# A ReLU² feed-forward behind an attention on one Trainium2 core: batch 0's first z tiles moved from SBUF to SBUF, and a new order of work

## The chip, the cores and the metric

The kernel runs on one core of one Trainium2 chip. The metric is the time of one execution on the device in microseconds (us). A profile of one execution stands beside the times; in it PE is the matrix engine (TensorE), PEld its weight loads, DVE is VectorE, ACT is ScalarE, POOL is GpSimd and SP is SyncE, which here only issues DMAs.

## The reference

There are 8 batches (b) with 8 heads each, a sequence of 512 tokens and 32 state rows per head, head size 64. Each head's x attends to the state, and the state attends to x; both results go through one feed-forward of width 512 → 2048 → 512 with a squared ReLU.

```python
scores = scale * x @ state.T;   a  = softmax(scores);   xread = a @ state      # 512 rows a head
scores2 = scale * state @ x.T;  a2 = softmax(scores2);  sread = a2 @ x         # 32 rows a head
x = concat([xread, sread])          # per batch 544 rows of 8*64 = 512
out = (maximum(x @ w_in, 0) ** 2) @ w_out
```

The weights come as 64-bit floats: the kernel reads them as pairs of 32-bit words and makes 32-bit floats of them on the chip.

## The kernel before

Everything that PE multiplies in quantity is split into a high and a low part (`_hi`, `_lo`), and a product is three matmuls: high by high, high by low, low by high. One matmul with 512 columns is the unit of the long run.

For the 512 token rows of a batch, `xread @ w_in` is not formed from xread. The state rows are multiplied into w_in first: `z = state @ w_in`, and then `h = a @ z`. So there are these pieces of work:

- **Weights.** `w_tile(fc)` loads one of 16 tiles of w_in (512 KB, `w_raw`) and `singles` makes `wi` of it; `wo_tile(fc)` does the same for w_out (`wo_raw`, `wof`) and splits the result into `wo_hi`, `wo_lo`. All raw tiles share four buffers (tag `raw`). `singles` takes one ACT instruction (L355) and three DVE instructions (L359, L364, L370) for a tile of 128x512.
- **Scores.** `scores(b, g)` for the two groups g of a batch: batches 0 and 1 in plain 32-bit matmuls (`sq`, L569, with the padded state `sp_f` that `pad` makes), the others with split x (`xt_hl`, `pq`, L590). A softmax on DVE, ACT and POOL follows, then `a_hi` and `a_lo`. In batches 0 and 1 PE turns tiles over (`sT`, `pa`).
- **z.** `z_part(k, g)` makes z for batches 0 to 3 and 256 columns of w_in: eight matmul records (`pz`, L471), two ACT copies to `z_stage`, one DMA from ACT's queue to `zd` in DRAM. `z_fetch(b, k)` reads a batch's z back with four DMAs on SP's queue (`z_raw`) and splits it into `z_hi`, `z_lo`. Only the first 256 columns of batch 0 go another way: `z_direct` (L495, `pzd`) multiplies the padded state with w_in again, straight into the layout that is needed. Batches 4 to 7 get theirs from `z_quad` (L441) and `zq`.
- **Up and down.** For each of the 16 columns tiles fc of a batch, `up` makes `ph` (six matmuls, L779), then ACT and DVE form r, the square and `g_hi`, `g_lo`; `down` adds twelve matmuls (L815) into four PSUM tiles `po`. Batch 0 is done in two visits (`PARTS`): fc 0 to 5, then all of batch 1, then the rest of batch 0.
- **Read.** `read(b, g)` makes the state rows' results (`pt`, `pr`, `sr`), and at the end 16 more `up` and `down` steps handle them.

Nothing is issued in the order of the code. Each piece is recorded with its engine, an assumed cost, its buffers and a due time, and `Planner` lays all of them out in an assumed timeline: an engine that comes free takes, of the pieces that could begin at once, the one that is due first. The order that comes of it is the fixed order of each engine's queue on the chip. `plan` computes due times backwards from the `up` and `down` steps, with a slack (`SLACKS`) on every step; `run` tries 16 such plans (four `FIRST` by four `SLACKS`) and keeps the one that ends first in its own account. A DMA waits at the head of its queue (SP's or ACT's) until its buffers are free, and what is queued behind it waits too.

`keep_busy(k)` is filler: four small matmuls on a constant tile (`warm`, written to a PSUM tile of tag `ph`). There are 40 of them (160 matmuls, L842); the planner puts them where PE would have nothing else in its account. On the chip they run wherever they stand.

Of the kernel before, what the change touches and what calls it, by code (L numbers as in the profile page):

```python
# [44 lines left out]
class Planner:  # L45


    RATE = 330.0
    NEAR = 1.0
    SLACKS = (1.0, 1.5, 2.0, 2.5)  # L50

    def __init__(self):
        self.ops, self.last_w, self.readers, self.chains = [], {}, {}, {}
        self.whens = []

    def op(
        self, engs, run, r=(), w=(), lat=0.2, due=1e9, begin=0.0, size=0, both=False, hold=None,
        chain=None, land=2.2, slack=0.3, unit=None,
    ):
# [75 lines left out]
    def plan(self, scale):  # L135
# [26 lines left out]
        while len(log) < len(self.ops):  # L162
# [80 lines left out]
def memory_attention_then_relu2_ffn(  # L243
# [77 lines left out]
    ]  # L321
    zd = [dr.tile([P, NG, HG, FW], F32, name=f"zd_{k}") for k in range(NFCH)]
# [25 lines left out]
    def singles(out_f, words, r, w):  # L348

        bits = lambda: out_f().bitcast(I32)  # L350
        high = lambda: words()[..., 1]
        low = lambda: words()[..., 0]
        n = 512
        op(
            act(n, 0.08), lambda e: nc.scalar.activation(out_f(), high().bitcast(F32), AF.Abs, scale=GUARD),  # L355
            r=r, w=w,
        )
        op(
            dve2(n), lambda e: nc.vector.tensor_scalar(  # L359
                out=bits(), in0=bits(), scalar1=3, scalar2=None, op0=ALU.logical_shift_left),  # L360
            r=w, w=w,
        )
        op(
            dve(n), lambda e: nc.vector.scalar_tensor_tensor(  # L364
                out=bits(), in0=high(), scalar=-0x80000000, in1=bits(),
                op0=ALU.bitwise_and, op1=ALU.bitwise_or),
            r=[*r, *w], w=w, both=True,
        )
        op(
            dve(n), lambda e: nc.vector.scalar_tensor_tensor(  # L370
                out=bits(), in0=low(), scalar=29, in1=bits(),
                op0=ALU.logical_shift_right, op1=ALU.bitwise_or),
            r=[*r, *w], w=w, both=True,
        )
# [56 lines left out]
    def z_quad(kq, g, q, w_hl, begin):  # L431
# [15 lines left out]
        op(("PE", 0.75), products, r=r, w=pz, begin=begin)  # L447
# [3 lines left out]
    def z_store(pz, stage, out, keys, part, order):  # L451
        for i in range(2):
            op(
                act(512), lambda e, i=i: nc.scalar.copy(out=part(i), in_=pz[i].t),
                r=[pz[i]], w=[(stage, i)],
            )
        load(
            out, lambda: stage.t.rearrange(order), 512,
            r=[(stage, 0), (stage, 1)], w=keys, eng="ACT", issue=0.35, hold=None, land=4.5,
        )  # L460

    def z_part(k, g):
# [3 lines left out]
        def product(e):  # L466
            for q in range(NQ):
# [41 lines left out]
    def z_fetch(b, k):  # L509
# [3 lines left out]
        for j in range(HG):  # L513
            load(
                lambda j=j: raw.t[j * N:(j + 1) * N], lambda j=j: src[:, :, j, :], 64,
                r=[("zd", b // GB, k, g, q) for g in range(NG) for q in range(NQ)], w=[(raw, j)], issue=0.62, hold=30.0, chain="zf",
            )
# [9 lines left out]
    def pad(b):  # L527
        pairs[b] = [tile_([P, NG, S], F32R, n) for n in ("a_hi", "a_lo")]
        src = stP[b].rearrange("p (g q n) -> p g q n", g=NG, q=2)
        rows = [slice(i * D, (i + 1) * D) for i in range(2)]  # L530
        at = [slice(i * N, (i + 1) * N) for i in range(2)]
        raw = tile_([P, NG, 2, N], F32, "sp_raw")
        load(lambda: raw.t, lambda: src, 64, w=[raw], due=1e9 if b else -60.0)
        for i in range(2):
            if b < PLAIN_X:
                if i == 0:
                    wide[b] = tile_([P, NG, 2, P + D], F32, "sp_f1", "x_hl") if b else sp_f
                    if b:
                        op(("POOL", 0.9), lambda e: nc.gpsimd.memset(wide[b].t, 0.0), w=[(wide[b], 0), (wide[b], 1)])
                op(  # L540
                    dve2(2 * N * NG), lambda e, i=i: nc.vector.tensor_copy(
                        out=wide[b].t[rows[i], :, :, at[i]], in_=raw.t[rows[i]]),
                    r=[raw], w=[(wide[b], i)],
                )
                continue
# [7 lines left out]

    def scores(b, g):
        xt = tile_([P, NQ, S], F32, "xt_raw", "xraw")
        load(
            lambda: xt.t, lambda: xT[b, g * CG:(g + 1) * CG, :].rearrange("(q p) s -> p q s", p=P),
            512, w=[xt], chain="x", due=1e9 if b else -12.0 + 4 * g, eng="SP" if b or g else "ACT",
        )
# [4 lines left out]
        if b < PLAIN_X:  # L564
            sq = tile_([P, S], F32, "sq", "px")

            def product(e):
                for q in range(NQ):
                    nc.tensor.matmul(  # L569
                        sq.t, lhsT=wide[b].t[:, g].rearrange("p q n -> p (q n)")[:, q * P:(q + 1) * P],  # L570
                        rhs=xt.t[:, q, :], start=q == 0, stop=q == NQ - 1,
                    )

            op(("PE", 1.77), product, r=[(wide[b], i) for i in range(2)] + [xt], w=[sq])
            pst = tile_([P, S], F32, "st")
            op(act(S), lambda e: nc.scalar.copy(out=pst.t, in_=sq.t), r=[sq], w=[pst])
        else:
            pst = tile_([P, S], F32, "st")
            for q in range(NQ):
# [3 lines left out]
                    [xt], [(hl, 0)], [(hl, 1)], engs=[gps(S)],  # L583
# [27 lines left out]
        turned = b < PLAIN_X  # L611
# [143 lines left out]
    def wo_tile(fc):  # L755
# [4 lines left out]
            w=[raw],  # L760
# [76 lines left out]
    def keep_busy(k):  # L837
# [6 lines left out]
        op(("PE", 0.4), product, w=[ph], begin=1.2 + 0.4 * k)  # L844
# [47 lines left out]
    for b, lo, hi in PARTS:  # L892
        if b not in started:
            pad(b)
            for g in range(NG):
                scores(b, g)
            started.add(b)
        if lo == 0 and b >= 1:
# [120 lines left out]
```

## Time and profile before

| | |
|---|---|
| median of 3 executions | 687.50 us (687.41 to 688.02) |
| profiled execution | 687.25 us, of it 685.5 us from the first to the last instruction (the span) |
| PE | 676.1 us busy, 99% of the span, granted clock 0.999 |
| DVE, ACT, POOL | 417.7, 398.1 and 158.4 us busy |
| DMA | 79.55 MB, on average 116 GB/s |

A row of a timeline gives start, duration, engine, source line and operation, tiles out<-in, and in brackets the engine's idle time ahead of it with what ended it. Matmuls overlap: a matmul of 512 columns has a duration of about 0.39 us, but the next one starts 0.23 us later, and it is this step from start to start that the sums use.

### The profile page before, as it was taken

To read this page: it belongs to the slowest core of one execution; us is meant where nothing else is said; L and a number is where in the kernel's file an instruction comes from. 1 tells how busy PE (TensorE), PEld (TensorE's weight loads), DVE (VectorE), ACT (ScalarE), POOL (GpSimd) and SP (SyncE) were. 2 spreads that over 40 slices of the span, in tenths; PEclk is the share of its full clock that TensorE was granted. 3 is DMA by queue.
4 is the path that set the end of the run, shared out by engine and by line. 5 is a ranking of instruction groups with operands and counts; after the bars stand their busy time and mean duration, and the time that the engine had idled before them with its cause. 6 is when DMAs were issued, how large, how long until landed. Compare 5 with 4: busy or idle time off the path is not lost.

```text
span 685.5 us, 9700 instructions
## 1 busy us (share of the span) xinstructions
PE 676.1 (99%) x3288; PEld 540.5 (79%) x3288; DVE 417.7 (61%) x716; ACT 398.1 (58%) x758; POOL 158.4 (23%) x175
## 2 busy tenths in 40 slices
PE   8999999999999999999999999999999999999997
PEld 6677777788878887777777888888888888888895
DVE  6999898475486666554454675775954444333532
ACT  4897778585555667565444665675754443334452
POOL 1010022233333444111210552354413210000000
PEclk9999999999999999999999999999999999999999
DMA  9967984451132213523242223221232112100101
GB/s 312 362 221 246 328 277 146 153 181 64 62 123 67 93 31 138 203 109 143 72 174 92 85 69 105 81 89 55 92 124 63 31 32 93 31 1 0 62 1 32
DMA packets 50609, 79.55 MB, mean 116 GB/s; under 512 B 6528, under 2 KB 32896, under 8 KB 50560
## 3 DMA queue, kind: packets, MB, share of 16 engines
q1 hardware_dynamic: 45488, 61.37, 27.7%
q10 hardware_dynamic: 5072, 17.57, 6.5%
q8 instruction: 26, 0.43, 0.3%
q14 instruction: 23, 0.19, 0.1%
HBM read 52.17 MB, written 26.74 MB: 115 GB/s over the span
## 4 chain that ended last, share of the span: by engine, by line
PE 90%; DVE 6%; DMA 2%; issue 1%; ACT 0%; SPq 0%; DVEq 0%; ACTq 0%
PE po L815 53%; PE ph L779 28%; PE pr L720 2%; PE pz L441 2%; PE pq L590 2%; PE pz L471 2%; PE pt L702 1%; DVE wi L364 1%; DVE wi L370 1%; DVE wi L359 1%; DMA w_raw<-w_in 1%; DMA xt_raw<-xT 1%; DMA z_raw<-zd 1%; DVE wof L364 0%; DVE wof L370 0%
## 5 line engine op out<-in xcount | busy, mean ns | idle before, releaser
L815 PE MATMUL po<-wo_hi,g_hi 128*128 128x512 f32 x544 | 218.0, 401 | 0.0
L815 PE MATMUL po<-wo_lo,g_hi 128*128 128x512 f32 x544 | 213.9, 393 | 0.0
L793 DVE TENSOR_TENSOR ph<-ph,r 128x512 f32<-128x512 f32 (+1 forms) x111 | 76.2, 686 | 197.5 <-ACT r L785 197.1
L815 PE MATMUL po<-wo_hi,g_lo 128*128 128x512 f32 x544 | 155.8, 397 | 0.0
L785 ACT ACTIVATE r<-ph 128x512 f32<-128x512 f32 (+1 forms) x144 | 82.7, 575 | 104.1 <-PE ph L779 103.5
L339 ACT CAST g_hi<-ph 128x512 fp32r<-128x512 f32 (+1 forms) x144 | 81.2, 564 | 99.6 <-PE po L815 94.5
L815 PEld LDWEIGHTS po<-wo_hi,g_hi 128*128 128x128 f32 x544 | 102.3, 188 | 28.1 <-issue 7.3
L815 PEld LDWEIGHTS po<-wo_lo,g_hi 128*128 128x128 f32 x544 | 102.4, 188 | 20.8 <-issue 0.2
L815 PEld LDWEIGHTS po<-wo_hi,g_lo 128*128 128x128 f32 x544 | 99.6, 188 | 22.6 <-issue 2.4
L344 DVE TENSOR_TENSOR g_lo<-ph,g_hi 128x512 fp32r<-128x512 f32 (+1 forms) x144 | 94.0, 653 | 29.2 <-PE po L815 21.9
L344 POOL TENSOR_TENSOR xn_hl<-xn_raw,xn_hl 128x512 fp32r<-128x512 f32 x32 | 44.2, 1381 | 175.9 <-ACT xn_hl L339 147.4
L779 PE MATMUL ph<-a_hi,z_hi 128*128 128x512 f32 x256 | 80.5, 395 | 1.2 <-DVE g_lo L344 1.2
L779 PE MATMUL ph<-a_hi,z_lo 128*128 128x512 f32 x256 | 80.1, 394 | 0.0
L779 PE MATMUL ph<-a_lo,z_hi 128*128 128x512 f32 x256 | 79.1, 390 | 0.0
L779 PEld LDWEIGHTS ph<-a_hi,z_hi 128*128 128x128 f32 x256 | 47.8, 188 | 12.4 <-ACT wo_hi L339 1.5
L779 PEld LDWEIGHTS ph<-a_lo,z_hi 128*128 128x128 f32 x256 | 48.0, 188 | 11.4
L779 PEld LDWEIGHTS ph<-a_hi,z_lo 128*128 128x128 f32 x256 | 48.0, 188 | 11.3
L344 DVE TENSOR_TENSOR z_lo<-z_raw,z_hi 128x512 fp32r<-128x512 f32 x63 | 48.6, 772 | 2.0 <-ACT z_hi L339 1.5
L344 POOL TENSOR_TENSOR xt_hl<-xt_raw,xt_hl 128x512 fp32r<-128x512 f32 x24 | 32.9, 1370 | 62.3 <-ACT xt_hl L339 62.3
L339 ACT CAST z_hi<-z_raw 128x512 fp32r<-128x512 f32 x63 | 38.8, 616 | 1.8 <-DMA z_raw<-zd 1.6
L649 POOL TENSOR_TENSOR q<-q,s 128x512 f32<-128x512 f32 x13 | 13.7, 1051 | 66.1 <-DVE s L644 45.8
L339 ACT CAST xn_hl<-xn_raw 128x512 fp32r<-128x512 f32 x32 | 19.8, 619 | 12.1 <-PE pr L720 9.4
(137 smaller groups left out, 753.2 us busy)
## 6 DMA issues: line engine op xcount, KB each, us to landing
w_raw<-w_in SPq DMA_DIRECT2D x16, 512.0 KB, 5.9
wo_raw<-w_out SPq DMA_DIRECT2D x16, 512.0 KB, 5.4
zd<-z_stage ACTq DMA_DIRECT2D x16, 512.0 KB, 4.5
xn_raw<-xn SPq DMA_DIRECT2D x16, 512.0 KB, 4.2
zq<-zq_stage ACTq DMA_DIRECT2D x16, 512.0 KB, 2.9
z_raw<-zq SPq DMA_DIRECT2D x128, 64.0 KB, 2.5
z_raw<-zd SPq DMA_DIRECT2D x124, 64.0 KB, 2.5
xt_raw<-xT SPq DMA_DIRECT2D x15, 512.0 KB, 3.7
```

What stands on the lines that cost most here:

```text
L339: act(n, 0.03 if both else 0.0), lambda e: nc.scalar.copy(out=hi(), in_=src()),
L344: lambda e: ENGINE[e].tensor_sub(out=lo(), in0=src(), in1=hi().bitcast(F32)),
L359: dve2(n), lambda e: nc.vector.tensor_scalar(out=bits(), in0=bits(), scalar1=3, scalar2=None, op0=ALU.logical_shift_left),
L441: nc.tensor.matmul(pz[i].t, lhsT=s_hl.t[own, m, g * NQ + q, :], rhs=w_hl[w].t[own, :, q, :], start=j == 0, stop=j == 2,)
L471: nc.tensor.matmul(pz[i].t[:, q, :], lhsT=st[0].t[own, cc, :], rhs=wi[own, k * FPC:(k + 1) * FPC, cc, :], start=True, stop=True,)
L590: nc.tensor.matmul(pq.t, lhsT=sp_hl[:, g, q].rearrange("p i n -> p (i n)"), rhs=hl.t[:, i], start=i == 0, stop=i == 1,)
L649: two_source(S, b), lambda e: ENGINE[e].tensor_mul(out=q1.t, in0=q1.t, in1=s1.t.broadcast_to([P, NJ, N])),
L720: nc.tensor.matmul(pr.t[:, q].rearrange("p i c -> p (i c)"), lhsT=eh.t[:, t, q].rearrange("p i n -> p (i n)"), rhs=hl.t[:, t].rearrange("p ...
L779: nc.tensor.matmul(ph.t[:, :width], lhsT=w, rhs=v, start=j == 0, stop=j == len(pairs_) - 1)
L785: act(width), lambda e: nc.scalar.activation(rl.t[:, :width], ph.t[:, :width], AF.Relu),
L793: nc.vector.tensor_mul(out=ph.t[:, :width], in0=ph.t[:, :width], in1=rl.t[:, :width])
L815: nc.tensor.matmul(po[t].t, lhsT=(g[0], g[0], g[1])[j].t[:, t * P:(t + 1) * P], rhs=wo[k][j % 2][:, i, :], start=first and j == 0, stop=la ...
```

## The change

- **z.** `DIRECT = 0`: `z_direct` is no longer called. For the first six column tiles (`NEAR_Z`, k = 0, 1, 2) `z_part` sends batch 0's 32 rows from `z_stage` straight to `z_raw` in SBUF, with four DMAs for each of the two groups on SP's queue, and stores only the other 96 rows to `zd`.
- **Weights.** `singles` takes the three lowest bits from a byte of the low word: ACT scales the high word in place (L398), one instruction on DVE or ACT makes the low bits (L407 or L405), and two DVE instructions put the parts together (L412, L418). In the built order 10 of the 32 byte instructions stand on DVE and 22 on ACT.
- **x.** Batch 0's group 0 comes in two halves of 256 KB on two queues. Batch 1's padded state is loaded straight into `sp_f` (runs of 128 bytes) instead of through `sp_raw` and two DVE copies.
- **Filler.** 88 pieces (352 matmuls) instead of 40 (160).
- **Planner.** Other assumed costs (`RATE`, `LAT`, the costs of `z_part`, `z_quad`, landing times), one plan instead of 16, PE's results ready for PE at once, and `SHIFTS`, a table that moves the due times of some kinds of pieces that are due in the first 150 us.

```diff
 class Planner:
-    RATE = 330.0
+    RATE = 350.0
     NEAR = 1.0
-    SLACKS = (1.0, 1.5, 2.0, 2.5)
+    LAT = {"DVE": 0.12, "ACT": 0.14}
+    SLACKS = (2.5,)
+    EARLY = 150.0
+    SHIFTS = {
+        ("a_lo", 1): (1.7, 0.0),
+        ("po", 1): (2.2, 0.0),
...
+        for o in self.ops:
+            if o.due < self.EARLY and o.kind in self.SHIFTS:
+                more, slope = self.SHIFTS[o.kind]
+                o.due += more + slope * max(o.due, -30.0)
...
-                s_.ready = max(s_.ready, o.end)
+                s_.ready = max(s_.ready, end if e == "PE" == s_.engs[0][0] else o.end)
...
-    DIRECT = 2
+    DIRECT = 0
+    NEAR_Z = 6
     PLAIN_X = 2
-    WARM = 40
+    TURNED = 2
+    WARM = 88
+    COLD = 8
...
-    START, FIRST, STEP = 8.0, (3.0, 3.5, 4.0, 4.4), 4.4
+    START, FIRST, STEP = 8.0, (3.5,), 4.4
...
-            act(n, 0.08), lambda e: nc.scalar.activation(out_f(), high().bitcast(F32), AF.Abs, scale=GUARD),
-            r=r, w=w,
-        )
-        op(
-            dve2(n), lambda e: nc.vector.tensor_scalar(
-                out=bits(), in0=bits(), scalar1=3, scalar2=None, op0=ALU.logical_shift_left),
-            r=w, w=w,
+            act(n, 0.08), lambda e: nc.scalar.activation(
+                high().bitcast(F32), high().bitcast(F32), AF.Copy, scale=GUARD),
+            r=high_r, w=high_r,
+        )
+        def top_bits(e):
+            if e == "ACT":
+                nc.scalar.activation(bits(), top(), AF.Copy, scale=1 / 32, bias=-15.5 / 32)
+            else:
+                nc.vector.tensor_scalar(
+                    out=bits(), in0=top(), scalar1=1 / 32, scalar2=-15.5 / 32, op0=ALU.mult, op1=ALU.add)
+        op([dve(n), act(n, 0.08)], top_bits, r=low_r, w=w)
...
+        near = N if DIRECT <= k * FPC < NEAR_Z else 0
+        z_store(pz, stage, lambda: zd[k][near:, g].rearrange("p h f -> p (h f)"),
+                [("zd", 0, k, g, q) for q in range(NQ)], lambda i: stage.t[:, :, i, :], "p q i f -> p (q i f)", near)
+        if near:
+            if not g:
+                near_z[k] = tile_([P, NG, FW], F32, "z_raw")
+            raw = near_z[k]
+            for j in range(HG):
+                load(
+                    lambda j=j: raw.t[j * N:(j + 1) * N, g], lambda j=j: stage.t[:N, j // 2, j % 2, :], 32,
+                    r=[(stage, j % 2)], w=[(raw, g, j)], issue=0.5, hold=None, land=2.6,
+                )
+            if g == NG - 1:
+                hi, lo = z_pair(0, k)
+                split(...)
...
-        op(("PE", 0.4), product, w=[ph], begin=1.2 + 0.4 * k)
+        op(
+            ("PE", 0.4 if k < COLD else 0.21), product, w=[ph],
+            begin=1.2 + 0.4 * min(k, COLD) + 0.21 * max(0, k - COLD),
+        )
```

What the change does to the order shows at three places. The rows name line, operation and tiles; `x4` stands for four alike. First PE's queue just ahead of the first `up` (`ph<-a_hi,z_hi`). Before, in the middle of the softmax of batch 0, with the direct z (`pzd`):

```order
L617 MATMUL sT<-ident,st 128x128 x4
L495 MATMUL pzd<-wi,sp_f 128x128 x4
L471 MATMUL pz_325<-wi,st_z 128x256
L471 MATMUL pz_326<-wi,st_z 128x256
```

After, the end of the last run of filler ahead of the first `up`:

```order
L942 MATMUL idle<-warm 128x128
L652 MATMUL sq<-xt_raw,sp_f_119 128x512 x4
L879 MATMUL ph<-a_hi,z_hi 128x512 x2
L879 MATMUL ph<-a_hi,z_lo 128x512 x2
L879 MATMUL ph<-a_lo,z_hi 128x512 x2
L519 MATMUL pz_641<-wi,st_z 128x256
L519 MATMUL pz_642<-wi,st_z 128x256
```

Both score products of batch 1 (`sq`, four rows) now stand ahead of the first `up`, one of them stood behind it; four parts of z and 220 matmuls of filler stand ahead of it, where there were three parts, the two `pzd` and 120.

Second, SP's queue of DMAs early on. Before and then after, from the last tiles of w_in (`w_raw`) that go ahead of the first z:

```order
L378 DMA w_raw<-w_in 128x1024
L378 DMA wo_raw<-w_out 128x1024 x3
L378 DMA xn_raw<-xn 128x4x256
L378 DMA wo_raw<-w_out 128x1024 x2
L378 DMA z_raw<-zd_100 32x2x256 x4
```

```order
L426 DMA w_raw<-w_in 128x1024
L426 DMA z_raw<-z_stage 32x256 x4
L426 DMA wo_raw<-w_out 128x1024
L426 DMA z_raw<-z_stage 32x256 x4
L426 DMA wo_raw<-w_out 128x1024 x2
```

The first z of batch 0 now goes through SP's queue, two tiles of w_out wait behind its eight small DMAs, and the first read-back from DRAM comes later.

Third, PE's queue around the last score product (`pq`) ahead of batch 5. Before, then after:

```order
L590 MATMUL pq<-xt_hl,sp_hl 128x512 x2
L815 MATMUL po_3719<-wo_hi_91,g_hi 128x512
L815 MATMUL po_3719<-wo_lo_92,g_hi 128x512
L815 MATMUL po_3724<-wo_hi_91,g_hi 128x512
L815 MATMUL po_3724<-wo_lo_92,g_hi 128x512
```

```order
L690 MATMUL pq<-xt_hl,sp_hl 128x512 x2
L879 MATMUL ph<-a_hi,z_hi 128x512 x2
L879 MATMUL ph<-a_hi,z_lo 128x512 x2
L879 MATMUL ph<-a_lo,z_hi 128x512 x2
L915 MATMUL po_3705<-wo_hi_95,g_hi 128x512
```

`wo_hi_91` holds the column tiles 8 and 9 of w_out, `wo_hi_95` the tiles 12 and 13: the product stood in the middle of batch 4 and now stands shortly before its end. Behind it, up to the first `up` of batch 5, stood 56 `po`, 24 `ph`, 8 `pt` and 8 `pr`; now there are 36 `po`, 12 `ph`, 8 `pt`, 4 `pr` and 40 matmuls of filler. The same happens at every batch from 2 on.

More of the change, by code (lines that the diff above doesn't have):

```diff
@@ L12 @@
 I32 = mybir.dt.int32
+U8 = mybir.dt.uint8
 AF = mybir.ActivationFunctionType
@@ L321, in memory_attention_then_relu2_ffn @@
     ]
+    sd = {
+        (b, g): dr.tile([P, S], F32, name=f"sd_{b}_{g}") for b in range(TURNED, PLAIN_X) for g in range(NG)
+    }
     zd = [dr.tile([P, NG, HG, FW], F32, name=f"zd_{k}") for k in range(NFCH)]
@@ L366, in singles @@
                 op0=ALU.bitwise_and, op1=ALU.bitwise_or),
-            r=[*r, *w], w=w, both=True,
-        )
-        op(
[L370 to L373, printed above, removed]
+            r=[*high_r, *w], w=w, both=True,
         )
@@ L457, in z_store @@
         load(
-            out, lambda: stage.t.rearrange(order), 512,
-            r=[(stage, 0), (stage, 1)], w=keys, eng="ACT", issue=0.35, hold=None, land=4.5,
+            out, lambda: stage.t[skip:].rearrange(order), 4 * (P - skip),
+            r=[(stage, 0), (stage, 1)], w=keys, eng="ACT", issue=0.35, hold=None, land=3.3,
         )
@@ L515, in z_fetch @@
                 lambda j=j: raw.t[j * N:(j + 1) * N], lambda j=j: src[:, :, j, :], 64,
-                r=[("zd", b // GB, k, g, q) for g in range(NG) for q in range(NQ)], w=[(raw, j)], issue=0.62, hold=30.0, chain="zf",
+                r=[("zd", b // GB, k, g, q) for g in range(NG) for q in range(NQ)], w=[(raw, j)], issue=0.62, hold=30.0, chain="zf", land=2.6,
             )
@@ L527, in pad @@
     def pad(b):
-        pairs[b] = [tile_([P, NG, S], F32R, n) for n in ("a_hi", "a_lo")]
         src = stP[b].rearrange("p (g q n) -> p g q n", g=NG, q=2)
@@ L531, in pad @@
         at = [slice(i * N, (i + 1) * N) for i in range(2)]
+        if 0 < b < PLAIN_X:
+            if b == 1:
+                wide[1] = tile_([P, NG, 2, P + D], F32, "sp_f1", "x_hl")
+                wide[1].hot = False
+                op(("POOL", 0.9), lambda e: nc.gpsimd.memset(wide[1].t, 0.0), w=[(wide[1], 0), (wide[1], 1)])
+            for i in range(2):
+                load(
+                    lambda i=i: wide[1].t[rows[i], :, :, at[i]], lambda i=i: src[rows[i]], 32,
+                    w=[(wide[1], i)], issue=0.62, hold=None, begin=6.0,
+                )
+            wide[b] = wide[1]
+            return
         raw = tile_([P, NG, 2, N], F32, "sp_raw")
@@ L534, in pad @@
         for i in range(2):
[L535 to L539, printed above, removed]
+            if not b:
+                wide[0] = sp_f
                 op(
                     dve2(2 * N * NG), lambda e, i=i: nc.vector.tensor_copy(
-                        out=wide[b].t[rows[i], :, :, at[i]], in_=raw.t[rows[i]]),
-                    r=[raw], w=[(wide[b], i)],
+                        out=sp_f.t[rows[i], :, :, at[i]], in_=raw.t[rows[i]]),
+                    r=[raw], w=[(sp_f, i)],
                 )
@@ L552, in two_source, with x_load, plain, product @@
         return [[dve(n)], [dve(n), gps(n)]][b] if b < 2 else [gps(n)]
-    def scores(b, g):
[L555 to L559, printed above, removed]
+    def x_load(b, g):
+        xt = tile_([P, NQ, S], F32, "xt_raw", "xraw")
+        src = xT[b, g * CG:(g + 1) * CG, :].rearrange("(q p) s -> p q s", p=P)
+        early = 0 < b < PLAIN_X
+        if b + g == 0:
+            for q in range(NQ):
+                load(
+                    lambda q=q: xt.t[:, q, :], lambda q=q: src[:, q, :], 256, w=[(xt, q)], chain="x",
+                    due=-62.0 + 6 * q, eng="SP" if q else "ACT",
+                )
+        else:
+            load(
+                lambda: xt.t, lambda: src, 512, w=[(xt, q) for q in range(NQ)], chain="x",
+                due=1e9 if b else -49.0, hold=None if early else 30.0, begin=6.0 if early else 0.0,
+            )
+        return xt
+    def plain(b, g):
+        xt = x_load(b, g)
+        sq = tile_([P, S], F32, "sq", "px")
+        def product(e):
+            for q in range(NQ):
+                nc.tensor.matmul(
+                    sq.t, lhsT=wide[b].t[:, g].rearrange("p q n -> p (q n)")[:, q * P:(q + 1) * P],
+                    rhs=xt.t[:, q, :], start=q == 0, stop=q == NQ - 1,
+                )
+        op(("PE", 1.77), product, r=[(wide[b], i) for i in range(2)] + [(xt, q) for q in range(NQ)], w=[sq])
+        pst = tile_([P, S], F32, "st", "st" if b < TURNED else "os_")
+        op(act(S), lambda e: nc.scalar.copy(out=pst.t, in_=sq.t), r=[sq], w=[pst])
+        if b >= TURNED:
+            load(lambda: sd[b, g], lambda: pst.t, 256, r=[pst], w=[("sd", b, g)], hold=None)
+        return pst
+    def scores(b, g):
+        if not g:
+            pairs[b] = [tile_([P, NG, S], F32R, n) for n in ("a_hi", "a_lo")]
         q1 = tile_([P, NJ, N], F32, "q1")
@@ L563, in scores @@
         s2 = tile_([P, 1], F32, "s2")
[L564 to L574, printed above, removed]
+        if b < TURNED:
+            pst = plain(b, g)
+        elif b < PLAIN_X:
             pst = tile_([P, S], F32, "st")
-            op(act(S), lambda e: nc.scalar.copy(out=pst.t, in_=sq.t), r=[sq], w=[pst])
+            load(lambda: pst.t, lambda: sd[b, g], 256, r=[("sd", b, g)], w=[pst])
         else:
+            xt = x_load(b, g)
             pst = tile_([P, S], F32, "st")
```

68 lines of the change are left out of this document (54 added, 14 removed).

## The prediction

> **What bounds the kernel now.** I read the page first, then the table of windows, PE's waits, and PE's timeline at both ends. The page says that PE never rests and that the last chain is PE's:
>
> ```profile
> span 685.5 us, 9700 instructions
> ...
> PE 676.1 (99%) x3288; PEld 540.5 (79%) x3288; DVE 417.7 (61%) x716; ACT 398.1 (58%) x758; POOL 158.4 (23%) x175
> ...
> PE 90%; DVE 6%; DMA 2%; issue 1%; ACT 0%; SPq 0%; DVEq 0%; ACTq 0%
> ```
>
> Busy is not useful, though. The windows (columns PE, PEld, DVE, ACT, POOL, then the granted clock) show why the start is slower than the rest:
>
> ```profile
> 8.00:16.00 8.00, 6.76 (x65) 5.02 (x64) 7.97 (x17) 4.56 (x10) 0.00 (x0) 1.00 1.05 338
> ...
> 24.00:32.00 8.00, 7.56 (x41) 5.27 (x40) 7.97 (x17) 7.33 (x16) 0.00 (x0) 1.00 1.03 348
> ...
> 140.00:200.00 60.00, 60.00 (x272) 48.91 (x271) 38.11 (x67) 36.54 (x70) 21.55 (x23) 1.00 0.31 99
> ```
>
> In the first rows DVE is full (7.97 of 8) and so are the DMA engines (1.05); after 140 us PE alone is full. What the whole loses by waiting is little:
>
> ```profile
> PE ph L779 <- DVE g_lo L344: 1.2, 1, 1.2
> PE sq L569 <- DMA xt_raw<-xT: 1.0, 2, 0.5
> ...
> PE pz L471 <- DVE wi L370: 0.7, 1, 0.7
> PE pzd L495 <- DVE wi L370: 0.4, 1, 0.4
> ```
>
> So the time is the sum of what stands in PE's queue, filler included, plus a few us of waits. The change is therefore costed as a sum over that queue, in two stretches that meet at the first `up`:
>
> ```profile
> 0.99 3.60 PE L842 MATMUL idle<-warm 128*128 128x128 bf16 x32 [0.99 <-DVE warm L314]
> 5.11 1.95 PE L569 MATMUL sq<-xt_raw,sp_f 128*128 128x512 f32 x4 [0.52 <-DMA xt_raw<-xT]
> 6.90 0.83 PE L842 MATMUL idle<-warm 128*128 128x128 bf16 x12
> ...
> 8.29 1.73 PE L842 MATMUL idle<-warm 128*128 128x128 bf16 x28
> ...
> 15.54 1.06 PE L495 MATMUL pzd<-wi,sp_f 128*128 128x128 f32 x8
> 16.53 1.13 PE L471 MATMUL pz<-wi,st_z 64*128 64x256 f32 x8
> 17.59 0.65 PE L658 MATMUL pa<-ident,q 128*128 128x128 f32 x4
> 18.09 0.61 PE L842 MATMUL idle<-warm 128*128 128x128 bf16 x8
> ...
> 25.69 0.71 PE L779 MATMUL ph<-a_hi,z_hi 128*128 128x512 f32 x2
> ...
> 680.61 0.40 PE L842 MATMUL idle<-warm 128*128 128x128 bf16 x4
> ```
>
> Prices, from start to start: a score product `sq` 6.90 − 5.11 = 1.79; a part of z 17.59 − 16.53 = 1.06; four turns (`pa`, `sT`) 18.09 − 17.59 = 0.50; a `pzd` 16.53 − 15.54 = 0.99; a filler matmul (1.73 − 0.83) / (28 − 12) = 0.056, but for the first 32, which take 3.60. First `up` at 25.69, last product done at 680.61: 654.9 between them.
>
> **The change, part by part. Up to the first `up`.** The queue now holds 220 filler matmuls, four `sq`, four parts of z, four sets of turns, no `pzd`. The first product cannot begin before its x is there: 5.11 stands for that, and I leave it, since the two halves are the same 512 KB ahead of the same weights. The work behind it: 4 × 1.79 = 7.2, 4 × 1.06 = 4.2, 4 × 0.50 = 2.0, (220 − 32) × 0.056 = 10.5, together 23.9; the first `up` cannot begin before 29.0. I add 0.5 for waits inside, since the fourth part of z needs PSUM that ACT has to empty first; the bounds are 0 and 1.7, what the waits for x, `wi` and again `wi` in the table above came to (0.5 + 0.7 + 0.4), rounded up. That makes 29.5, against 25.69. It is not all lost: one `sq` and one part of z (2.9) are done that were not done before.
>
> Do the suppliers keep up with 29.5? The rows that price them, of DVE, ACT, SP's queue, and the DMAs (on the page, and in the DMA view of 14 to 36 us, when the queues are full; the last column is us to landing):
>
> ```profile
> 6.97 0.43 DVE L359 TENSOR_SCALAR wi<-wi 128x512 int32<-128x512 int32 x1 [2.72 <-ACT wi L355]
> ...
> 8.32 0.68 DVE L364 SCALAR_TENSOR_TENSOR wi<-w_raw,wi 128x512 int32<-128x512 int32 x1
> 8.91 0.42 DVE L359 TENSOR_SCALAR wi<-wi 128x512 int32<-128x512 int32 x1
> ...
> 17.69 1.07 ACT L454 COPY z_stage<-pz 128x512 f32<-128x512 f32 x2 [0.17 <-PE pz L471]
> ...
> 26.68 2.95 SPq L378 DMA_DIRECT2D z_raw<-zd  x4
> ...
> z_raw<-zd SPq DMA_DIRECT2D x124, 64.0 KB, 2.5
> ...
> z_raw<-zd SPq DMA_DIRECT2D x4, 64.0 KB, 6.0
> ```
>
> DVE begins on weights at 6.97. From its first instruction there to the first `z_lo` the new queue has 29 instructions with a step of 0.6 (8.91 − 8.32) and four of 0.2: 18.2, so 25.2, if nothing waits. The z from SBUF to SBUF is an operation that the trace lacks; the nearest are the read-backs of z, 2.5 to 6.0 to landing. I take 6.0, since the queue is full then. ACT had the second part of z in `z_stage` at 17.69 + 1.07 = 18.8; four issues put the last 2.3 later; 18.8 + 2.3 + 6.0 + 1.3 for high and low = 28.4. So the route from SBUF to SBUF lies beside PE's queue with 1.1 to spare; the filler is its cover, and I cost it at nothing. Two tiles of w_out wait behind its DMAs on SP's queue; the first `down` wants them 3 us and more after the first `up`. The 128-byte loads of `sp_f` replace two copies of 0.2 on DVE and have until 25 to land.
>
> **The weights.** The forms that come nearest:
>
> ```profile
> L359 DVE TENSOR_SCALAR wof<-wof 128x512 int32<-128x512 int32 x6 | 2.5, 419 | 0.0
> ...
> L364 DVE SCALAR_TENSOR_TENSOR wof<-wo_raw,wof 128x512 int32<-128x512 int32 x6 | 4.1, 685 | 0.0
> ...
> L355 ACT ACTIVATE wof<-wo_raw 128x512 f32<-128x512 f32 x6 | 4.0, 671 | 0.3 <-DMA wo_raw<-w_out 0.3
> ```
>
> The byte instruction lies between 0.42 and 0.69 on DVE; I take 0.69, as its operands are strided, and 0.67 on ACT. DVE sheds 32 × 0.42 and gains 10 × 0.69: 6.5 less. ACT gains 22 × 0.67 = 14.7. DVE's saving reaches the end only where PE waited for DVE; that is in the waits below. ACT has room (4.56 to 7.33 of 8), but its copies free the PSUM of the parts of z; what that can cost is the second term of the waits.
>
> **From the first `up` to the last product.** Before 654.9. Off: 2.9 for what moved ahead. Filler: 36 matmuls stood here (160 less 120 ahead and 4 behind), 2.0; now there are 44, 40 of them ahead of batch 5: +2.5. Waits that stood here: the wait for `g_lo` (1.2 and 0.2 of run-up), 0.4 for the first `wo_lo`, and parts of z that waited for their second PSUM tile:
>
> ```profile
> 66.74 1.61 PE pz L471 x8
> ...
> 71.78 1.06 PE pz L471 x8
> ...
> 103.04 1.31 PE pz L471 x7
> ```
>
> A free one takes 1.06; three took 0.5, 0.5 and 0.25 more: 1.2. All of it together 3.0, and no row says that any of it must stay, so I take it out and put new waits in as a term of their own. 654.9 − 2.9 − 2.0 + 2.5 − 3.0 = 649.5; the last product would end at 29.5 + 649.5 = 679.0.
>
> **The tail.** Behind it now stand 88 filler matmuls: 88 × 0.056 + 0.2 = 5.1. The rest that hid four of them is 685.47 − 680.61 = 4.9 long (copies, stores). So the filler ends last, by 0.2: span 684.1.
>
> **New waits.** (1) Scores come late at every batch from 2 on. Between the last score product and the first `up` of the batch stand, in the new queue, 66, 61, 45, 48, 67 and 67 matmuls of `up` and `down`, and some others (24 of z's at batch 4, turns and 40 of filler at batch 5); at the step of 1.39 / 6 = 0.23 of the next rows, and the prices above, that is 15.7, 14.1, 14.3, 14.7, 15.9 and 15.9 us:
>
> ```profile
> 582.24 1.39 PE ph L779 x6
> 583.63 2.76 PE po L815 x12
> ...
> 255.21 0.63 PE L590 MATMUL pq<-xt_hl,sp_hl 128*128 128x512 f32 x2
> ...
> 271.18 1.30 POOL L344 TENSOR_TENSOR a_lo<-at,a_hi 128x512 fp32r<-128x512 f32 x1 [2.16 <-ACT a_hi L339]
> ...
> 393.71 0.63 PE L590 MATMUL pq<-xt_hl,sp_hl 128*128 128x512 f32 x2
> ...
> 405.62 1.75 POOL L344 TENSOR_TENSOR a_lo<-at,a_hi 128x512 fp32r<-128x512 f32 x1
> ```
>
> From the end of that product to the end of the last `a_lo` it took 272.48 − 255.84 = 16.6 for batch 4 and 407.37 − 394.34 = 13.0 for batch 5 (start and duration of these rows); the other four lie between, at 13.1 to 14.2. `a_lo` is needed 0.9 after the first matmul of the `up`. At 13.0 nothing waits anywhere. At 16.6 the six wait 0, 1.6, 1.4, 1.0, 0 and 0: 4.0. Five of the six rows are near 13.5, so I take 0.5. (2) The parts of z: 12 remain, three of 13 waited; between 0 and 1.2, I take 0.6. (3) Others such as the 1.4 and 0.4 above: 0 to 1.8, I take 0.2, since the suppliers lead. Together 1.3 of 0 to 7.0.
>
> 684.1 + 1.3 = 685.4; with the 1.8 that lie around the span (687.25 − 685.47) 687.2. The median of the executions is 0.2 above the profiled one: 687.4.
>
> **Rivals.** *Nothing waits again* (0.22). For it speaks that the new queue has no filler between the first `up` and the middle of batch 4, so the planner saw PE covered throughout. Then the head takes 29.0, no wait is added: 684.1 − 0.5 = 683.6, as a time 685.4 to 686.1.
>
> *The scores come too late* (0.22), the case on the other side. Before, the gap between `pq` and `up` was never under 20 us; now it is 14 to 16, and POOL and ACT hold other work in that stretch. It decides from 15.0 us on at batch 3. At 16.6 everywhere it costs 4.0 instead of 0.5: 690.9; at 15.6, about 1.4: 688.3.
>
> *The first z comes late* (0.08). If the small DMAs take 10 us in the full queue instead of 6, high and low are ready at 32.4, not 28.4, and the first `up` begins 2.9 later: 690.3. It decides from 7.1 us to landing on. No wait for one thing in PE's table is longer than 1.2, and the granted clock was 1.00 in all windows. [...]
>
> *Filler that only stands in for waits* (part of the forecast): if PE would have waited at batch 5 anyway, its 2.2 are not a loss of the filler, but they are spent all the same.
>
> **How the numbers follow.** A measurement of this kernel tells a change from none at about 0.2%, 1.4 us: faster is under 686.1, slower over 688.9. The forecast, 687.4 with its own range 686.1 to 688.9, gets 0.48. Faster is the first rival, 0.22. Slower gets 0.30: the late scores, the late z. The range takes in the low end of the first rival and the late scores near their upper bound: 685.4 to 690.8.
>
> **What would show it.** Right: first `up` at 29 to 30; no `pzd`; 88 filler matmuls behind the last `po`, and PE the last to end; PE's waits under 2 us in all; about 2 us of filler ahead of batch 5. Wrong: a wait of PE for ACT's `a_hi` or POOL's `a_lo` at the batches; a wait for `z_hi` at the first `up`; byte instructions of over 0.7 us, or ACT full up to 64 us, so that parts of z wait for `z_stage` copies; a step of the filler other than 0.056.

## The result and the profile after

The changed kernel is slower: 696.32 us median of 4 executions (694.34 to 698.44) against 687.76 (687.41 to 691.03), ratio 1.011, interval 1.007 to 1.016. The forecast was 687.4, its range ended at 690.8. The profiled execution took 696.23. The page after, span, busy time and chain:

```profile
span 694.4 us, 10050 instructions
...
PE 686.0 (99%) x3464; PEld 551.8 (79%) x3464; DVE 415.7 (60%) x695; ACT 406.0 (58%) x775; POOL 156.5 (23%) x175
...
PE 90%; DMA 5%; DVE 2%; ACT 1%; POOL 1%; SPq 0%; issue 0%; ACTq 0%; DVEq 0%; POOLq 0%
```

In the chain, DVE's 6% became 2%, and DMA's 2% became 5%: the start is no longer set by DVE's work but by landings. The span is 8.9 us longer, and the table of PE's waits has new first lines:

```profile
PE sq L652 <- ACT z_stage L502: 1.9, 1, 1.9
PE pa L758 <- POOL q L749: 1.8, 2, 1.6
...
PE pz L519 <- ACT z_stage L502: 0.9, 2, 0.6
PE sT L717 <- ACT st L659: 0.8, 1, 0.8
```

PE's timeline shows the three places: the start, a stretch near 55 us, and the end.

```profile
29.83 3.70 PE L652 MATMUL sq<-xt_raw,sp_f 128*128 128x512 f32 x8 [1.90 <-ACT z_stage L502]
32.97 1.02 PE L879 MATMUL ph<-a_hi,z_hi 128*128 128x512 f32 x2
...
53.66 0.66 PE L758 MATMUL pa<-ident,q 128*128 128x128 f32 x4 [0.20 <-POOL q L749]
55.91 0.94 PE L758 MATMUL pa<-ident,q 128*128 128x128 f32 x4 [1.60 <-POOL q L749]
...
57.08 0.63 PE L915 MATMUL po<-wo_lo,g_hi 128*128 128x512 f32 x1
57.50 0.63 PE L915 MATMUL po<-wo_hi,g_hi 128*128 128x512 f32 x1
...
687.45 0.39 PE L915 MATMUL po<-wo_hi,g_lo 128*128 128x512 f32 x1
687.68 5.09 PE L942 MATMUL idle<-warm 128*128 128x128 bf16 x88
```

The first `up` is at 32.97 (forecast 29.5). From there to the last product (687.45 + 0.39 = 687.84) it is 654.87 (forecast 649.5 and waits of 1.3). Behind it come 694.4 − 687.84 = 6.6 (forecast 5.1). So 3.5, 4.1 and 1.5 us are to be explained. Around 57 us a matmul of `down` starts 0.42 us after the one ahead of it (57.50 − 57.08) where 0.23 is usual.

The windows (PE, PEld, DVE, ACT, POOL, granted clock, DMA share, GB/s) say whose lack it is:

```profile
24.00:32.00 8.00, 5.50 (x42) 3.46 (x40) 4.42 (x11) 4.93 (x10) 0.00 (x0) 1.00 0.71 223
...
50.00:60.00 10.00, 8.20 (x33) 6.28 (x32) 7.79 (x15) 8.63 (x20) 2.51 (x2) 0.83 0.44 145
```

From 24 to 32 us PE, DVE and ACT are idle for 31 to 45% of the time (PE's 5.50 hold filler, too), and the DMAs move 223 GB/s, where before the change it was 348. No engine is full, and neither are the DMAs: what is missing must have been issued late. The DMA view of 14 to 36 us, of before and after the change, gives the same in bytes:

```profile
DMA packets 3251, 7.92 MB, mean 360 GB/s; under 512 B 295, under 2 KB 1496, under 8 KB 3248
```
```profile
DMA packets 2324, 5.60 MB, mean 254 GB/s; under 512 B 447, under 2 KB 958, under 8 KB 2321
...
z_raw<-z_stage SPq DMA_DIRECT2D x16, 32.0 KB, 4.0
```

SP's timeline and SP's waits of 14 to 36 us show what held the issues:

```profile
16.18 2.86 SPq L426 DMA_DIRECT2D z_raw<-z_stage  x4
19.13 0.53 SPq L426 DMA_DIRECT2D wo_raw<-w_out  x1
22.54 3.13 SPq L426 DMA_DIRECT2D z_raw<-z_stage  x4
```
```profile
SPq L426 <- DMA zd<-z_stage: 2.8, 1, 2.8
SPq L426 <- DMA wo_raw<-w_out: 1.8, 2, 1.1
```

The last row of ACT's timeline that writes the second part of z into `z_stage` stands well ahead of that:

```profile
17.77 1.07 ACT L502 COPY z_stage<-pz 128x512 f32<-128x512 f32 x2
```

The part was there at 17.77 + 1.07 = 18.84, but SP issues its copies only at 22.54, and the wait is put down to the landing of a store of the *first* part to DRAM, with which they have nothing to do. The built order, with the semaphores that each instruction waits for, has the reason (rows of SP, then of ACT):

```
14 L426 DMA w_raw_310<-w_in 128x1024 [waits DMAHW0_49,DVE_49,Activation_49]
15 L426 DMA z_raw_352<-z_stage_333 32x256 [waits DMAHW1_49,Activation_49]
16 L426 DMA z_raw_352<-z_stage_333 32x256 [waits DMAHW2_49]
17 L426 DMA z_raw_352<-z_stage_333 32x256 [waits DMAHW3_49,Activation_49]
18 L426 DMA z_raw_352<-z_stage_333 32x256 [waits DMAHW4_49]
19 L426 DMA wo_raw_395<-w_out 128x1024 [waits DMAHW5_49,DVE_49]
20 L426 DMA z_raw_352<-z_stage_393 32x256 [waits DMAHW7_49,Activation_49]
...
18 L426 DMA zd_0_99<-z_stage_333 96x1024 [waits DMAHW7_49,Activation_49]
```

In this order the DMAs of SP and ACT take eight semaphores in turn (`DMAHW0` to `DMAHW7`), and each waits until the last DMA on its own semaphore, the eighth before it, has landed. There are eight places here. The trace agrees: ACT's store on `DMAHW7` was issued at 16.67 and landed at 22.48, and the copy of SP that waits for `DMAHW7` was issued at 22.54. A copy of 32 KB holds one about as long as a load of 512 KB does (in the trace the four copies issued from 16.18 on landed after 4.7 to 6.5 us, the load of w_out behind them after 4.8), and the change put 24 such copies into the first 50 us. I call this the ring theory; the experiments test it.

### The profile page after: what moved, and what is told of

Read it like the earlier page. It is cut to its first block, busy times and chain, and to the rows that moved or that the text cites. A ratio compares the mean times of both kernels' runs of the same rounds, so it can differ in the third digit from the quotient of the medians.

```text
span 694.4 us, 10050 instructions
## 1 busy us (share of the span) xinstructions
PE 686.0 (99%) x3464; PEld 551.8 (79%) x3464; DVE 415.7 (60%) x695; ACT 406.0 (58%) x775; POOL 156.5 (23%) x175
## 4 chain that ended last, share of the span: by engine, by line
PE 90%; DMA 5%; DVE 2%; ACT 1%; POOL 1%; SPq 0%; issue 0%; ACTq 0%; DVEq 0%; POOLq 0%
PE po L915 53%; PE ph L879 28%; DMA w_raw<-w_in 3%; PE pr L820 2%; PE pz L519 2%; PE pz L489 2%; PE pq L690 2%; PE idle L942 1%; PE pt L802 1%; DMA xn_raw<-xn 1%; DMA wo_raw<-w_out 1%; DMA z_raw<-z_stage 1%; SPq L426 0%; POOL q L749 0%; DVE s L744 0%
## 5 line engine op out<-in xcount | busy, mean ns | idle before, releaser
L385 POOL TENSOR_TENSOR xn_hl<-xn_raw,xn_hl 128x512 fp32r<-128x512 f32 x32 | 42.0, 1311 | 267.6 <-ACT xn_hl L380 267.6
L749 POOL TENSOR_TENSOR q<-q,s 128x512 f32<-128x512 f32 x14 | 15.6, 1113 | 61.8 <-DVE s L745 61.1
L942 PEld LDWEIGHTS <-warm 128*128 128x128 bf16 x352 | 21.7, 103 | 3.9 <-issue 2.8
```

The lines of the kernel that those rows point to most:

```text
L385: lambda e: ENGINE[e].tensor_sub(out=lo(), in0=src(), in1=hi().bitcast(F32)),
L749: two_source(S, b), lambda e: ENGINE[e].tensor_mul(out=q1.t, in0=q1.t, in1=s1.t.broadcast_to([P, NJ, N])),
L942: nc.tensor.matmul(ph.t[:, t], lhsT=warm, rhs=warm, start=True, stop=True)
```

## The experiments

Rivals were that the bytes of the copies slow the DMAs, that ACT's queue is late through the byte instructions, and that the filler is the loss. To compare runs piece by piece, this table gives the time from one useful product of PE to another (starts in the traces, filler not counted, the first column from the span's start; the 40th lies near 20 us, the 100th after the first `up`, the 1300th and 1900th on both sides of the filler ahead of batch 5), and what follows the last `down`. "Part" is one of the six calls of `z_part` whose z goes by the small copies; two parts make a chunk:

| run | 0–40 | 40–100 | 100–200 | 200–400 | 1300–1900 | behind the last |
|---|---|---|---|---|---|---|
| changed kernel | 20.48 | 21.34 | 24.39 | 41.99 | 132.10 | 6.6 |
| after_again | 19.91 | 20.44 | 23.18 | 43.64 | 132.09 | 6.4 |
| one_per_part | 20.18 | 16.81 | 20.54 | 42.33 | 132.11 | 6.2 |
| gpsimd_queue | 20.33 | 18.84 | 20.54 | 44.86 | 132.23 | 6.2 |
| loads_by_gpsimd | 19.83 | 19.69 | 22.20 | 45.14 | 132.10 | 6.0 |
| no_late_filler | 19.47 | 21.43 | 23.99 | 43.66 | 130.30 | 4.6 |
| one_part_no_filler | 20.02 | 16.81 | 20.54 | 43.58 | 130.30 | 4.8 |
| pool_copies | 19.93 | 16.80 | 20.54 | 42.75 | 130.29 | 4.6 |

**The changed kernel again.** 

> The changed kernel once more, as the control for the others. Its four executions so far spread over 694.3 to 698.4 us, so another profile should show which part of the stretch up to 60 us moves: the ring theory (below) expects the wait of PE for the turned scores near 53 us, and the half-rate stretch behind it, to vary with the landing of z, 0 to 4 us, and the first up at 32 to 34. If instead the time varies with the first up alone, the two are one chain.

695.36 us, ratio 1.010 (1.007 to 1.013). First `up` at 31.27, the same waits:

```profile
PE sq L652 <- ACT z_stage L502: 1.9, 1, 1.9
PE pa L758 <- POOL q L749: 1.7, 2, 1.3
```

but this time the granted clock was 1.00 from 50 to 60 us. So the two late places are steady, the half-rate stretch is not. The first `up` fell a little outside the 32 to 34 expected.

**One DMA for each part.** 

> The copy of a part of batch 0's z from SBUF to SBUF is one DMA of 128 partitions in place of four of 32, same bytes, every engine's order unchanged; its rows are not the right ones, so batch 0's z is wrong and only the time counts. Ring theory (each DMA waits for the eighth before it to land, so small pieces use up places that loads need): the second copy is issued near 19 instead of 22.5 us, first up at 29.3 to 30.5, no wait of over 0.5 us for the turned scores near 53 us: 688 to 690.5 us. Rivals (bytes on the DMA engines; ACT's queue, late through the byte instructions): nothing that they name is changed, first up at 32.5 to 33.5, 694 to 697 us.

```diff
-for j in range(HG):
-    dma(raw.t[j * N:(j + 1) * N, g], stage.t[:N, j // 2, j % 2, :])
+dma(raw.t[:, g], stage.t[:, 0, 0, :])      # in the place of the fourth
```

688.05 us, ratio 1.001 (0.998 to 1.003): 7.3 us less, as the ring theory had it, and as fast as before the change. Its timeline, windows, and from the DMA views of 14 to 36 and of 15 to 19 us:

```profile
29.41 1.02 PE L886 MATMUL ph<-a_hi,z_hi 128*128 128x512 f32 x2
```
```profile
24.00:32.00 8.00, 8.00 (x52) 5.13 (x54) 7.18 (x15) 7.74 (x15) 0.00 (x0) 1.00 0.98 340
50.00:60.00 10.00, 10.00 (x50) 7.26 (x49) 10.00 (x16) 9.97 (x20) 1.29 (x1) 1.00 0.67 237
```
```profile
DMA packets 3394, 7.62 MB, mean 346 GB/s; under 512 B 481, under 2 KB 1712, under 8 KB 3391
...
z_raw<-z_stage SPq DMA_DIRECT2D x2, 128.0 KB, 6.0
```

The same engines' order, the same bytes, a quarter of the DMAs: the first `up` is at 29.41, both waits are gone, the DMAs carry 7.62 MB again. Bytes and ACT's byte instructions fall as causes. The table places the gain: 40–100 and 100–200. It does not come from faster landings: the second part's one DMA was issued at 18.08 and landed at 24.33, 6.3 us later, where the changed kernel's four were issued from 22.54 on and landed by 28.5. Besides the places, the run saves the issuing of three DMAs a part, and its DMA reads the first of ACT's two copies to `z_stage` alone, which is 0.5 us earlier.

**The copies from GpSimd's queue.** 

> The 24 small copies are issued from GpSimd's queue in place of SP's, their values and all other order unchanged. Ring theory: GpSimd's DMAs do not take the eight places that SP and ACT share, so the weight loads behind them go out at once and the second part's copies are issued as soon as ACT has written them; first up at 29.5 to 31.5, 688 to 692 us, unless one issue on GpSimd takes over 1.2 us, which would give the gain back. Rivals (bytes; ACT's queue): 694 to 697 us.

```diff
-op(("SP", 0.5), lambda e: nc.sync.dma_start(...))
+op(("SP", 0.5), lambda e: nc.gpsimd.dma_start(...))   # same place in the order
```

692.45 us, ratio 1.0046 (1.003 to 1.006), a little above the 688 to 692 expected. An issue took 0.50 on GpSimd. 100–200 is as with one DMA, 40–100 keeps 2.0 of its 4.5, with the first `up` at 30.59. In the DMA view of 16 to 21 us:

```profile
z_raw<-z_stage POOLq DMA_DIRECT2D x8, 32.0 KB, 5.7
```

The copies hold no place of the others now (in this run's built order they take eight semaphores of their own, `DMASW0` to `DMASW7`), and go out at once: the second part's from 18.57 on, the last of them landed at 25.86. They take 5.7 us to land, as the one DMA of a part did with 6.0, so the landing is not what this run has more than one_per_part. What it has more, by these rows, is the issuing of three further copies (1.5 from the first issue to the last) and the 0.5 above. Until they land the copies also hold the two buffers of `z_stage` (PE waited 3.0 for `z_stage` in four places).

**The loads from GpSimd's queue instead.** 

> The changed kernel with its 24 small copies on SP as they are and all its filler, but the six first loads of w_out and the six stores of batch 0's parts of z are issued by GpSimd's queue, outside the eight places. This parts two readings: if the places are what costs, the copies of the second part are issued by 22.2 instead of 25.1 us and the first up comes at 29.5 to 31.5, 689 to 692 us; if it is SP's time to issue 24 copies (0.6 each), which stays, the first up stays at 31.3 to 33.4, 694 to 696 us.

694.35 us, ratio 1.009 (1.007 to 1.011). For the start the reading by places held: the copies of the second part were issued from 18.46 to 21.6 with no standstill, and the first `up` came at 30.41, with SP's 16 issues as they were. The total did not follow it: it lies over 2 us above the 689 to 692 of that reading, where the other one had it, and can't be told from the changed kernel's 1.010. The table says where the gain went: the third chunk was late again (22.20 in 100–200, with one DMA 20.54), and 200–400 took 45.14, where the changed kernel had 41.99, with a wait of PE for `z_stage` of 1.3 at 75.4 and half the granted clock from 78.8 to 82.2. The DMA view of 39.4 to 44.2 us, and a wait of PE:

```profile
z_raw<-z_stage SPq DMA_DIRECT2D x4, 32.0 KB, 5.7
```
```profile
PE pa L758 <- POOL q L749: 1.1, 1, 1.1
```

So for the first `up` the places are shown to be a part: 2.6 of the 3.6 us by which it is later than in one_per_part in the one profile of the changed kernel, 0.9 of 1.9 in the other. The 1.0 that remain there against one_per_part go with SP's issuing time, unchanged here (2.5 from the second part's first issue to its last, landed at 26.0), and the 0.5 above; for the third chunk the two are not parted.

**The late filler left out.** 

> The 44 filler matmuls of the middle and the 88 behind the last product are left out, all other order unchanged. As the sum had it, the tail is then as before the change (4.7 us behind the last product against 6.6): 1.9 less; and of the 2.2 of filler ahead of batch 5 all go, if nothing else is late there: together 4.1 less, 692 us. Rival: the filler of the middle stands in a wait that would be there anyway (the scores of batch 5): 1.9 less only, 694.4.

 

> One DMA per part as in one_per_part (batch 0's z is wrong), and the 44 and 88 filler matmuls of the middle and the end left out. With the start undisturbed this prices the late filler: tail 4.7 us behind the last product in place of 6.2, and the 2.5 ahead of batches 4 and 5 gone: 684.0 us. Rival (the filler of the middle stands where PE would wait for the scores of batch 5 anyway): 686.5 us, with a wait of 1 to 2.5 us at the first up of batch 5.

 

> All values right: the small copies from GpSimd's queue, and the late filler left out. If the two prices add, 692.5 less 4.0: 688.4 us; if the late filler only stands in for waits, 691.

In all three the filler groups behind the 55th are not emitted; nothing else moves. no_late_filler: 692.83 us, 1.0064 (1.004 to 1.009), where the changed kernel had 1.010. one_part_no_filler: 685.2, 0.9971 (0.996 to 0.998), where one_per_part had 1.0008. gpsimd_no_filler: 688.59, 1.0019 (1.0005 to 1.003), where gpsimd_queue had 1.0046. By ratios that is 1.9 to 2.5 us in each pair, not the 4.0. (That 688.59 lies at the 688.4 expected is luck: the kernel before, run beside it, was 1.1 shorter as well, 687.09 against 688.20.) The table has the terms: 1.8 in 1300–1900 (2.5 expected; the wait for `a_lo` at batch 5 that shows up in its place is 0.2), 1.1 to 2.0 behind the last product (5.1 us are left in gpsimd_no_filler; 1.5 to 1.9 were expected). The rest is 200–400, which differs from run to run by up to 3 us, with waits of parts of z for `z_stage` (0 to 2.0): a spread that my expectations had left out.

**z as it was.** 

> All values right: the changed kernel with batch 0's z as it was before (two direct z, the rest through DRAM), no small copies, no late filler; halves of x, the byte instructions and the planner's new numbers stay. Ring theory: the loss comes from the small copies alone, so the rest of the change may show what it gives. By prices of before's rows the first up comes at 26.3, the two direct z cost 2.0 that the changed kernel does not have, 24 filler matmuls fewer stand ahead: 683.5 to 686 us. Rival (the byte instructions on ACT or the new order lose time by themselves): 688 us or more, with waits of PE for z_stage copies or z_hi of over 2 us in all.

689.67 us, ratio 1.004 (1.0025 to 1.006): missed by 4 to 6, on the side of the rival. The first `up` came at 27.14, but its waits are many small ones:

```profile
PE po L915 <- ACT g_hi L380: 1.1, 1, 1.1
...
PE pa L758 <- POOL q L749: 0.8, 1, 0.8
PE pz L519 <- ACT z_stage L502: 0.8, 1, 0.8
PE sT L717 <- ACT st L659: 0.7, 1, 0.7
```

Here the planner laid the whole order anew, so this run changes more than the z. It says that the rest of the change, in this order and without the late filler, does not gain but costs 0.4%, so the small copies are not all that loses time. Why these waits come is left open.

**The byte instructions alone.** 

> The kernel before with the new weight instructions alone (low bits from a byte on DVE or ACT; the planner lays the order anew, with 148 filler matmuls ahead of the first up in place of 120). DVE's saving lies beside PE's queue but for the 1 to 2 us of waits near the first up, and 28 filler more cost 1.6: 687 to 690 us. If the byte instructions on ACT were what made the changed kernel late: 692 or more.

687.58 us, ratio 1.0006 (0.9995 to 1.002): no change, as expected. The weights' new instructions, with the order that the planner makes of them, neither cost nor give.

**Copies without DMA.** 

> All values right: the 24 small copies are made by GpSimd itself, as copies from SBUF to SBUF that shift partitions, with no DMA at all; late filler left out, all other order unchanged. Ring theory: no place is taken and no landing waited for, so the start runs as with one DMA per part, first up at 29 to 30, 684.5 to 686.5 us, faster than before. Rival: GpSimd's copies take over 1.2 us each or slow DVE's instructions beside them (DVE at 0.68 now), then z comes as late as by DMA: 688 us or more.

```diff
-nc.sync.dma_start(out=raw.t[j * N:(j + 1) * N, g], in_=stage.t[:N, j // 2, j % 2, :])
+nc.gpsimd.tensor_copy(out=raw.t[j * N:(j + 1) * N, g], in_=stage.t[:N, j // 2, j % 2, :])
```

685.2 us, ratio 0.9960 (0.9946 to 0.9974): with the next run the fastest that computes the reference, 0.4% ahead of the kernel before. In the changed kernel GpSimd had idled from 2.5 to 52.5 us; its copies read partitions 0 to 31 and write 32 j to 32 j + 31. The tile view of `z_raw`, 14 to 40 us (duration min/median/max), and the first `up`:

```profile
L536 POOL COPY z_raw<-z_stage x24: 388/472/764, 15.4 to 38.0; 32x256 f32<-32x256 f32 x24
```
```profile
29.17 1.03 PE L880 MATMUL ph<-a_hi,z_hi 128*128 128x512 f32 x2
```

A copy takes 0.47 where the DMA took 3.0 to 5.8, and needs no place. Against gpsimd_no_filler, which differs in nothing else, it is 0.6% by ratios: the price of four DMAs a part, issue and landing together. It is not the price of the landing alone: one_part_no_filler, whose DMAs took some 6 us to land, has 0.9971 (0.996 to 0.998), which can't be told from this 0.9960, and the table has the two alike up to the 200th product.

**Less filler ahead.** 

> As pool_copies, and the last 72 of the 220 filler matmuls ahead of the first up are left out as well (4.0 us of PE's queue). If the filler there is a loss, as my sum has it, the first up comes 3 to 4 us earlier, 681 to 682 us. Rival: it stands where PE would wait for the weights of the fourth part of z and for z itself (high and low at 26 to 28 us): less than 1.5 us gained, 684 or more, with waits of PE ahead of the first up, and perhaps a lower granted clock behind them.

685.94 us, ratio 0.9956 (0.994 to 0.997): the same as with it, so the rival holds. Its timeline and window, with the `sq` of pool_copies ahead of them:

```profile
26.07 3.67 PE L653 MATMUL sq<-xt_raw,sp_f 128*128 128x512 f32 x8
```
```profile
24.19 2.53 PE L519 MATMUL pz<-wi,st_z 64*128 64x256 f32 x8 [2.44 <-ACT z_stage L502]
26.79 6.05 PE L653 MATMUL sq<-xt_raw,sp_f 128*128 128x512 f32 x8
32.27 1.02 PE L880 MATMUL ph<-a_hi,z_hi 128*128 128x512 f32 x2
```
```profile
24.00:32.00 8.00, 7.75 (x15) 3.79 (x16) 6.74 (x14) 6.35 (x13) 5.06 (x8) 0.57 0.88 276
```

Where 4.0 of filler stood, PE waits 2.4 and then runs two `sq` at half rate (6.05 instead of 3.67). In this profile, of the slowest of ten executions (683.57 to 688.13), the first `up` is even 3.1 later than with the filler; the median says that it comes out even.

## Why the prediction was wrong

**The step that failed** is the one that cost the copies at nothing: "the route from SBUF to SBUF lies beside PE's queue with 1.1 to spare". It summed four issues (2.3), a landing (6.0) and high and low, from the moment at which the second part was in `z_stage`. Missing was the wait ahead of the issue, 22.54 − 18.84 = 3.7: 0.8 of it SP's issues ahead (the load of w_out, until 19.66), 2.9 the places that were taken. No row of before up to 36 us has that price, since small copies came only once there, four together; the built order of the changed kernel with its semaphores does show it. The other terms were together too long, which hid most of the wait: from the first issue to the start of `z_hi` it took 28.67 − 22.54 = 6.1, where the sum had 2.3 + 6.0 = 8.3. The DMAs, short of issued loads, moved only 107 GB/s then (DMA view of 22.5 to 25.7 us):

```profile
z_raw<-z_stage SPq DMA_DIRECT2D x4, 32.0 KB, 3.0
```

Where the loads did go out, in one_per_part, a copy took the 6.0 of the forecast.

On balance z was 1.6 late, as the timelines of ACT and DVE have it:

```profile
28.67 0.62 ACT L380 CAST z_hi<-z_raw 128x512 fp32r<-128x512 f32 x1 [2.23 <-DMA z_raw<-z_stage]
```
```profile
29.32 0.69 DVE L385 TENSOR_TENSOR z_lo<-z_raw,z_hi 128x512 fp32r<-128x512 f32 x1 [1.43 <-DMA wo_raw<-w_out]
```

`z_lo` ended at 30.0, not 28.4. The rest is ACT's queue: it stood at `z_hi` until 28.67, behind that were the copies of the fourth part to `z_stage` (whose buffer the copies of the second part held as long), PE waited 1.9 for them ahead of two `sq`, and the first `up` stood behind those. The prediction named what is queued on SP behind the copies, not what is queued on ACT behind `z_hi`.

**The second place was not in the sum at all**: 3.85 us from the 100th to the 200th product. The copies of the sixth part, the second of the third chunk, took 4.4 us to issue (from 43.78) and landed by 50.5. DVE's timeline has what stood behind them:

```profile
51.30 0.69 DVE L385 TENSOR_TENSOR z_lo<-z_raw,z_hi 128x512 fp32r<-128x512 f32 x1 [1.63 <-DMA wo_raw<-w_out]
51.92 0.17 DVE L744 TENSOR_SCALAR s<-s 128x16 f32<-128x16 f32 x1
```

`s` is part of batch 1's scores: GpSimd's `q` and PE's `pa` wait for it, 1.8 in all, and in this execution the half rate after it took another 1.4 (seven steps of 0.43 for 0.23). The releaser named in the first row is a load that DVE's work does not need; what it waited for is ACT's `z_hi` at 50.65, behind the copies' landing.

**The tail** was mis-sized by 1.5: I let the span end with the filler. The filler ended at 692.77, the last stores landed at 692.5 to 693.0, 3.6 to 3.8 after their issue where before the change it was 2.2 to 2.4 (last section), and the closing drains and semaphores of all engines took the rest, in the trace from 693.05 up to 694.4. Without the filler the tail is 4.6 to 5.1.

**What held.** With the copies' DMAs reduced to a quarter, the sum is met within 1.1 us at every joint: first `up` 29.41 (29.5), last product 679.49 (679.0 and 1.3, so 0.8 early), tail 6.2 (5.1), span 685.7 (685.4). That the span is met to 0.3 is partly luck, since the last two errors cancel. So the price of the head, the 2.9 moved ahead, the 3.0 of waits taken out and the suppliers' lead were right in sum. That all filler of the head is a loss, as the sum charges it, was not: without 72 of its matmuls the time came out even. The scores at the batch boundaries came in time: no wait of PE for `a_hi` or `a_lo` there is over 0.2 us, so the rival on the other side with 0.22 was the wrong one. The rival that came true is *the first z comes late*, given 0.08. Its place was right, its price (690.3) was not: it looked at the first z alone, and took the landing for the unknown, not the issue.

**The clock.** In the changed kernel the clock fell after waits of 0.2 and 1.6 us within 2.5 (granted 0.83 from 50 to 60 us), and in its second run it did not after 0.4 and 1.3 (1.00 there); nor did it, in either run, after the one wait of 1.9 at the first `sq` (1.00 from 24 to 40 us). In no_late_filler it fell after one of 2.1 (0.79 from 24 to 32), with less filler after one of 2.4 (0.57 from 24 to 32), and in loads_by_gpsimd 2.0 after one of 1.3 had ended. So by these runs the length of a wait alone does not tell whether half rate follows; what else decides is not shown. Nor is the wait that filler stands in for all that it can save: with less filler half rate followed the wait of 2.4.

**The landing.** The forecast's 6.0 came from read-backs of z. The copies from GpSimd took 5.7 beside the loads (gpsimd_queue, 389 GB/s), those from SP 3.0 (at 107 GB/s) to 5.8 (at 310), medians in their windows.

## What to carry to other kernels

Count DMAs, not bytes, where loads are issued ahead: with a fixed number of places, eight here, each small copy can keep a large load from going out, and the sign of it here was that DMAs and engines were idle together (223 GB/s instead of 348 from 24 to 32 us, with PE, DVE and ACT idle for 31 to 45%). One DMA in the place of four took as long to land (6.0 us, the four from GpSimd's queue 5.7), and got the 7.3 us back. A wait that is put down to an unrelated transfer, like the 2.8 us of SP here, is a hint at such a place; the built order with its semaphores shows it ahead of any run. When a transfer becomes late, follow every in-order queue that waits for it, and look whether an idle engine can do the move without a DMA; on GpSimd it took 0.47 us a copy.

## What was not expected of the hardware

With filler behind the last product the last stores landed 3.6 to 3.8 us after their issue (changed kernel, DMA view of 688.7 to 690), without it 2.2 to 2.4 (before the change, 681.7 to 682.7):

```profile
out<-os__6953 SPq DMA_DIRECT2D x2, 64.0 KB, 3.6
out<-os__6953 ACTq DMA_DIRECT2D x2, 64.0 KB, 3.8
```
```profile
out<-os__6814 SPq DMA_DIRECT2D x2, 64.0 KB, 2.2
out<-os__6814 ACTq DMA_DIRECT2D x2, 64.0 KB, 2.4
```

The five profiles with that filler have 2.9 to 3.8 for these stores, the eight without it 2.1 to 2.4; the reason is not shown.

And GpSimd's copies cost DVE little, which was full beside them (7.67 to 8.00 of each 8 us from 16 to 40): its instructions of 0.68 us took 0.67 to 0.88, and from 15 to 39 us 43 instructions kept it busy for 23.56, in one_part_no_filler 43 for 21.95. One of the longest, of pool_copies:

```profile
25.82 0.88 DVE L385 TENSOR_TENSOR z_lo<-z_raw,z_hi 128x512 fp32r<-128x512 f32 x1
```
